# A new hand-written order of 4711 steps, and some steps on their other engine, in a one-core kernel of pooled attention and a gated dense layer

## The chip, the cores and the metric

One core of a Trainium2 chip. The time is device microseconds of one execution; "the time" of a kernel is the median of three. The engines are TensorE (PE: matrix products; PEld is its weight load), VectorE (DVE), ScalarE (ACT), GpSimd (POOL) and SyncE (SP, which only starts transfers). Each works through its own queue in order and meets the others at semaphores.

## The reference

Attention over 8 batches and 8 heads of 576 queries of 64 columns. Keys and values are averaged over 8 neighbours first, so 72 are left of each. The result, 4608 tokens by 512, goes through a dense layer of 2048 columns with a sigmoid gate and back to 512.

```python
k_p = k.reshape(B, H, Sp, pool, D).mean(axis=3)
v_p = v.reshape(B, H, Sp, pool, D).mean(axis=3)
scores = scale * np.matmul(q, k_p.transpose(0, 1, 3, 2))
attn = np.exp(scores - np.max(scores, axis=-1, keepdims=True))
attn = attn / (np.sum(attn, axis=-1, keepdims=True) + 1e-09)
x = np.matmul(attn, v_p).transpose(0, 2, 1, 3).reshape(B * S, H * D)
h = x @ w_in
g = h * (1.0 / (1.0 + np.exp(-1.702 * h)))
out = g @ w_out
```

## The kernel before

**Numbers in two halves.** PE multiplies rounded operands. To keep the precision, an operand is split into a rounded part and the rest: a copy rounds it (`x`, `ah`, `gh`), a subtraction makes the rest (`x` again, `al`, `gl`). A product is then the sum of three matmuls. So most products on PE wait for a copy (ACT or DVE) and a subtraction (DVE or POOL).

**Tiles and stages.** Batch b's first 512 tokens are chunk b of the dense layer. Chunks 0 and 1 are computed directly: `h` (lines 1675 to 1677), gate `g`, `gh`, `gl`, and `o` (1717 to 1719), each step three matmuls of 512 columns. For chunks 2 to 6 pairs of weight blocks are used with combined operands (as in Strassen's scheme): `pair` makes products `ha` and `hb` of six matmuls of 256 columns (line 1880), copies an `ha` product out of its bank into `shared` or `gall` ("keep copy", `cs`, line 1895), adds (1902), applies the gate (1919, 1927), subtracts (`gl`, 1934), and `outputs` makes `o` (2086 to 2088), in steps of three matmuls again. Chunk 7 and the 64 tokens left of every batch come last: `hidden` (`la`, `lb`, `lc`, line 2155), sums and splits of the gate's results (`ou`, line 2332; `oa`, `ob`, `oc`, `od`, lines 2323 and 2326), `outgoing` (`m1` to `m7`, line 2386), and `combined`, which adds and stores.

**Attention beside it.** The attention of batch b+1 runs between the products of chunk b, in two pieces of 256 and 320 tokens and blocks of 128 of the 512 columns. For a piece: scores (line 1126), exponent, sums, weighing `sc` (1198), copies of the weights into `main` (1241) and `tail` (1232), a transpose of each on DVE (`mt`, 1341; `tt`, 1290), splits `ah`/`al` and `at` (1348, 1353, 1311, 1314), and the product with the values `pav` (1365 to 1368) into one of two PSUM banks. From the bank DVE or ACT read: a copy `xt` (1425), the rounded `x` (1413) and the rest `x` (1416). From the `xt` of the two pieces combinations are subtracted (`less`, 1457) and split (1463), the operands `x` and `xs` of the pair products. The pooled keys of the next batch come from a reduction `red` (908), `tred` (970), masks `kbd`, `tbd` (918, 980) and a product `kps` (1004). The weights' own splits and sums are `stage` (1787, 1790).

**The order.** All 4711 steps are made first. A string `ORDER` (lines 27 to 462) then names each once; `E:name` with E one of A (ACT), V (DVE), G (POOL), P (PE), D (load, started by SP), O (output transfer). A star in front puts the step on its other engine: a copy of ACT on DVE, a subtraction of POOL on DVE. So each engine's queue is the sequence of its tokens, and nothing is reordered behind that:

```python
for token in ORDER.split():
    engine, name = token.lstrip("*").split(":")
    t = named[f"{ENGINES[engine]} {name}"]
    assert t.before <= done, t.name
    if token[0] == "*":
        t.swap()
    placed.append(t)
    done.add(t)
```

A name like `ha5_3#1` is the second `ha` step of chunk 5's pair 3; `x2_0#0` is block 0 of batch 2, first piece (`2_0`) or second (`2_1`), of the attention.

Of the kernel before, what the change touches and what calls it, by code (L numbers as in the profile page):

```python
# [18 lines left out]
P = 128  # L19
# [22 lines left out]
P:h0_0#1 P:h0_0#2 A:w#6 P:h0_0#3 D:raw#18 P:h0_0#4 A:w#3 P:h0_0#5 A:e#10 V:nm0_1#2 G:raw#8 V:sc0_1#1 V:e#10  # L42
A:qt0_1#3 A:raw#10 G:w#6 P:h0_0#6 G:w#3 P:h0_0#7 V:raw#10 V:sc0_1#2 P:sps0_1#3 A:w#8 P:h0_0#8 P:h0_0#9 A:sc0_1#0
P:h0_0#10 A:g0_0#0 D:raw#22 P:h0_0#11 V:nm0_1#3 V:sc0_1#3 D:qr1_0#7 P:h0_0#12 V:sps0_1#0 P:h0_0#13 *A:gh0_0#0
G:raw#7 G:w#8 G:raw#10 *G:gl0_0#0 D:raw#21 A:sc0_1#1 *A:w#10 P:h0_0#14 D:qr1_0#5 *A:w#5 D:kv1_0#1 G:w#10 P:h0_0#15
D:raws#2 V:sps0_1#1 P:h0_0#16 A:g0_0#1 V:sps0_1#2 V:main0_1#1 P:h0_0#17 A:gh0_0#1 G:w#5 P:h0_0#18 A:e#9 D:tl1#0
D:raws#1 A:raw#9 P:h0_0#19 V:tail0_1#0 A:w#7 P:o0_0#0 P:o0_0#1 V:main0_1#0 P:h0_0#20 V:main0_1#2 D:raw#19 P:h0_0#21
P:h0_0#22 P:tpt0_1#0 P:apt0_1#0 G:gl0_0#1 P:o0_128#0 P:o0_128#1 D:kv1_0#0 V:e#9 A:ah0_1#0 A:at0_1#1 V:raw#9
*A:at0_0#1 A:e#11 D:raw#26 P:apt0_1#1 A:ah0_1#1 G:w#7 A:raw#11 P:h0_0#23 A:g0_0#2 V:main0_1#3 P:pav0_1#0 V:e#11
# [2487 lines left out]
```

## Time and profile before

| | us |
|---|---|
| median of three runs (877.99 to 878.96) | 878.79 |
| span of the profiled execution | 876.5 |
| PE busy | 867.8 |
| DVE busy | 712.3 |
| ACT busy | 529.5 |
| POOL busy | 318.0 |

The profiled span lies 2.3 us under the median of the timed runs, which count a little time on either side of it. The granted clock of PE is 1.00 in nearly every slice of the span. A PE row's length is that of one matmul or of a run of like ones, whose ends overlap the next; so a lost fraction of a microsecond shows in the distance between starts, and only a longer one in "idle before". DVE, ACT and POOL rows give length and start of each instruction.

### The profile page before, as it was taken

How to read it: one execution, taken by the hardware profiler on the slowest of the kernel's cores; microseconds unless marked ns; L12 is line 12 of the kernel's file. 1: busy time of each engine (PE TensorE's matmuls, PEld its weight loads, DVE VectorE, ACT ScalarE, POOL GpSimd, SP SyncE). 2: the span in 40 equal slices, each digit the busy share in tenths (PEclk: the TensorE clock that was granted, in tenths of full speed). 3: DMA queues.
4: the chain of work that ended last, by engine and by line, in shares of the span. 5: the costliest groups of instructions: out<-in, count | busy, mean ns of one | idle time of the engine just before them, and what ended most of it. 6: DMA issues, size and time to landing. Idle time of an engine off the chain costs nothing.

```text
span 876.5 us, 15636 instructions
## 1 busy us (share of the span) xinstructions
PE 867.8 (99%) x5322; PEld 775.8 (89%) x5322; DVE 712.3 (81%) x1413; ACT 529.5 (60%) x1170; POOL 318.0 (36%) x325
## 2 busy tenths in 40 slices
PE   8999999999999999999999999999999999999998
PEld 7889888888898999998999999999999988889998
DVE  6999988897879896788887877788878866778887
ACT  4987855547565774767566755677476743455430
POOL 2778753554321113222522242324522123432321
PEclk9999999999999999999999999999999999999999
DMA  9966444576577666756785777667766457978003
GB/s 275 377 219 185 131 133 162 167 228 199 173 226 218 213 209 211 232 159 209 239 245 160 219 215 231 191 200 213 213 200 194 155 182 217 332 230 298 1 13 85
DMA packets 146351, 174.31 MB, mean 199 GB/s; under 512 B 85216, under 2 KB 97504, under 8 KB 146272
## 3 DMA queue, kind: packets, MB, share of 16 engines
q1 hardware_dynamic: 141808, 165.32, 61.1%
q10 hardware_dynamic: 4464, 8.00, 2.5%
q8 instruction: 42, 0.69, 0.3%
q14 instruction: 37, 0.30, 0.1%
HBM read 141.95 MB, written 31.33 MB: 198 GB/s over the span
## 4 chain that ended last, share of the span: by engine, by line
PE 92%; SPq 2%; DVE 2%; DMA 2%; ACT 1%; issue 0%; POOL 0%; POOLq 0%; DVEq 0%; ACTq 0%
PE ha L1880 13%; PE hb L1880 10%; PE m L2386 9%; PE o L2086 8%; PE o L2087 8%; PE o L2088 8%; PE la L2155 5%; PE sps L1126 4%; PE h L1677 3%; PE h L1675 3%; PE h L1676 3%; PE o L1717 3%; PE o L1718 3%; PE o L1719 3%; PE lc L2155 2%; PE lb L2155 1%
## 5 line engine op out<-in xcount | busy, mean ns | idle before, releaser
L1934 POOL TENSOR_TENSOR glall<-shared,ghall 128x256 fp32r<-128x256 f32 x78 | 61.6, 795 | 200.2 <-ACT shared L1927 137.7
L2086 PE MATMUL o<-w,ghall 128*128 128x512 f32 x320 | 127.1, 397 | 0.0
L2087 PE MATMUL o<-w,ghall 128*128 128x512 f32 x320 | 126.2, 394 | 0.0
L2088 PE MATMUL o<-w,glall 128*128 128x512 f32 x320 | 124.9, 390 | 0.0
L2088 PEld LDWEIGHTS o<-w,glall 128*128 128x128 f32 x320 | 60.1, 188 | 13.8 <-DVE glall L1934 0.2
L1880 PE MATMUL ha<-xs,ws 128*128 128x256 f32 x480 | 70.9, 283 | 0.0
L1934 POOL TENSOR_TENSOR glall<-gall,ghall 128x256 fp32r<-128x256 f32 x43 | 33.4, 782 | 102.4 <-ACT gall L1927 73.1
L1880 PEld LDWEIGHTS ha<-xs,ws 128*128 128x128 f32 x480 | 66.2, 190 | 4.4 <-ACT gall L1895 0.2
L1880 PE MATMUL hb<-x,ws 128*128 128x256 f32 x480 | 67.1, 283 | 0.0
L2086 PEld LDWEIGHTS o<-w,ghall 128*128 128x128 f32 x320 | 60.6, 189 | 6.4
L2087 PEld LDWEIGHTS o<-w,ghall 128*128 128x128 f32 x320 | 60.6, 190 | 5.8
L1880 PEld LDWEIGHTS hb<-x,ws 128*128 128x128 f32 x480 | 63.3, 190 | 2.4
L1919 ACT ACTIVATE ghall<-shared 128x256 fp32r<-128x256 f32 x108 | 43.8, 416 | 34.8 <-DVE shared L1902 15.7
L1675 PE MATMUL h<-x,w 128*128 128x512 f32 (+1 forms) x160 | 57.5, 359 | 0.0
L1705 POOL TENSOR_TENSOR gl<-g,gh 128x512 fp32r<-128x512 f32 x27 | 36.6, 1354 | 57.3 <-ACT gh L1697 49.0
L1676 PE MATMUL h<-x,w 128*128 128x512 f32 (+1 forms) x160 | 55.5, 347 | 0.0
L1677 PE MATMUL h<-x,w 128*128 128x512 f32 (+1 forms) x160 | 55.5, 347 | 0.0
L1241 ACT COPY main<-sc 32x256 f32<-32x256 f32 (+2 forms) x109 | 48.6, 446 | 4.9 <-DVE sc L1198 2.5
L1902 DVE TENSOR_TENSOR shared<-shared,hb 128x256 f32<-128x256 f32 x81 | 33.4, 413 | 22.2 <-PE hb L1880 18.5
L1895 ACT COPY shared<-ha 128x256 f32<-128x256 f32 x63 | 23.3, 369 | 42.4 <-PE ha L1880 42.1
L1126 PE MATMUL sps<-k,qt 128*128 128x144 f32 x320 | 45.9, 287 | 0.0
L1717 PE MATMUL o<-w,gh 128*128 128x512 f32 x112 | 45.4, 405 | 0.0
(270 smaller groups left out, 2430.6 us busy)
## 6 DMA issues: line engine op xcount, KB each, us to landing
ws<-wd SPq DMA_DIRECT2D x144, 512.0 KB
shared<-wd SPq DMA_DIRECT2D x48, 256.0 KB
wd<-stage SPq DMA_DIRECT2D x16, 512.0 KB
raw<-in_moe_w_in_dram SPq DMA_DIRECT2D x15, 512.0 KB
raw<-in_moe_w_out_dram SPq DMA_DIRECT2D x15, 512.0 KB
kv_False<-in_k_dram SPq DMA_DIRECT2D x28, 256.0 KB
kv_True<-in_v_dram SPq DMA_DIRECT2D x28, 256.0 KB
out_dram<-osb ACTq DMA_DIRECT2D x28, 256.0 KB
```

The costliest lines, as they stand in the source:

```text
L1126: nc.tensor.matmul(ps()[:, t * PW : (t + 1) * PW], lhsT=qt()[:, s0 : s0 + P], rhs=m.k2()[:, jj], start=True, stop=True,)
L1675: nc.tensor.matmul(o, lhsT=w[:, 0, j], rhs=xs[:, 0], start=j == 0, stop=False)
L1676: nc.tensor.matmul(o, lhsT=w[:, 1, j], rhs=xs[:, 0], start=False, stop=False)
L1677: nc.tensor.matmul(o, lhsT=w[:, 0, j], rhs=xs[:, 1], start=False, stop=j == NJ - 1)
L1717: nc.tensor.matmul(o, lhsT=gh()[:, i, tok], rhs=w[:, 0], start=f == 0, stop=False)
L1880: nc.tensor.matmul(o, lhsT=wv()[:, r, jj], rhs=xo(k, jj), start=start and n == 0, stop=n == len(terms) - 1,  skip_group_check=not start,)
L1934: engine.tensor_tensor(out=gl(), in0=part(i), in1=gh().bitcast(F32), op=ALU.subtract)
L2086: nc.tensor.matmul(o(), lhsT=gh()[:, tok], rhs=w()[:, 0], start=start, stop=False)
L2087: nc.tensor.matmul(o(), lhsT=gh()[:, tok], rhs=w()[:, 1], start=False, stop=False)
L2088: nc.tensor.matmul(o(), lhsT=gl()[:, tok], rhs=w()[:, 0], start=False, stop=stop)
L2155: nc.tensor.matmul(bank(), lhsT=wv()[:, r, jj], rhs=xs[jj]()[:, k], start=start and n == 0, stop=n == len(terms) - 1, skip_group_check=not ...
L2386: nc.tensor.matmul(banks[i]()[:, i], lhsT=av(r)[:, i * P : (i + 1) * P], rhs=tv(k), start=p == 0 and n == 0 and (i == 0 or banks[0] is not ...
```

## The change

The string `ORDER` is replaced. The first 420 tokens are the same ones; from there on nearly every queue has a new order, though few steps move far: of PE's 1205 steps 438 keep their place and the rest move by up to 13 places, on DVE by up to 29, on ACT by up to 47, on POOL by up to 4; of the 653 loads 114 keep their place, the others move by up to 31. The stars change too: steps on DVE go from 1389 to 1377, on ACT from 1110 to 1085, on POOL from 319 to 356. All code but the string is the same, and since the string is seven lines shorter, line numbers behind it are smaller by 7 in the new file. A line of the diff, from each side:

```diff
-P:qps0_0#3 P:sps0_0#2 V:e#2 D:kv0#6 D:kv0#7 D:q0_2#0 A:raw#2 A:qt0_0#3 V:sc0_0#1 V:raw#2 D:q0_1#1 P:sps0_0#3 A:e#4
+P:sps0_0#2 V:e#2 D:kv0#6 D:kv0#7 D:q0_2#0 A:raw#2 A:qt0_0#3 V:sc0_0#1 V:raw#2 D:q0_1#1 P:sps0_0#3 A:e#4 D:q0_1#0
```

Three places, as the engines' queues stand before and now.

DVE around batch 2, beginning with the copy `xt` of the second `pav` product; before:

```order
L1425 COPY xt2_0_2499<-pav2_0_1_2469 128x256
L1241 COPY main2_1_2518<-sc2_1_2292 32x3x4x2x16 x2
L908 TENSOR_REDUCE red3_k0_2537<-kv3_0_False_2109 128x128
L1416 TENSOR_TENSOR x2_2465<-pav2_0_1_2469,x2_2465 128x256
L1241 COPY main2_1_2518<-sc2_1_2292 32x4x2x16
L1353 TENSOR_TENSOR al2_0_2_2574<-mt2_0_2_2506,ah2_0_2_2566 128x256
L1416 TENSOR_TENSOR x2_2465<-pav2_0_0_2460,x2_2465 128x256
L918 TENSOR_TENSOR kbd3_2594<-red3_k0_2537,mask2i_84 128x256
L970 TENSOR_REDUCE tred3_1_2599<-tl3_1_2278 128x64
L1241 COPY main2_1_2518<-sc2_1_2292 32x4x2x16
L1290 STREAM_TRANSPOSE tt2_1_2620<-tail2_1_2516 64x320
```

and now, beginning with the same copy:

```order
L1418 COPY xt2_0_2500<-pav2_0_1_2476 128x256
L1346 TENSOR_TENSOR al2_0_2_2558<-mt2_0_2_2502,ah2_0_2_2556 128x256
L911 TENSOR_TENSOR kbd3_2566<-red3_k0_2519,mask2i_84 128x256
L963 TENSOR_REDUCE tred3_1_2568<-tl3_1_2299 128x64
L973 TENSOR_TENSOR tbd3_2373<-tred3_1_2568,mask4_86 128x256
L1406 CAST x2_2576<-pav2_0_3_2571 128x256
L1283 STREAM_TRANSPOSE tt2_1_2596<-tail2_1_2535 64x320
L1783 TENSOR_TENSOR stage_1742<-stage_1742 128x512
L1234 COPY main2_1_2523<-sc2_1_2269 32x4x2x16
L1409 TENSOR_TENSOR x2_2576<-pav2_0_3_2571,x2_2576 128x256
L1409 TENSOR_TENSOR x2_2472<-pav2_0_0_2467,x2_2472 128x256
```

The subtraction `x2<-pav2_0_0`, which reads the bank of the first `pav` product, stood right behind `al2_0_2`; it now stands eight instructions further on, behind `tt2_1`. The copy `xt2_0<-pav2_0_1`, the first row of both, has gone behind the reduction `red3`, the other subtraction `x` and four `main` copies.

PE around pair 3 of chunk 5: `ha` and `hb` products and `o` steps of three matmuls; before:

```order
L1880 MATMUL ha5_2_6541<-x5_6309,shared8_2524 128x256 x6
L2086 MATMUL o5_0_6380<-w1_4_727,ghall0_2892 128x512
L2087 MATMUL o5_0_6380<-w1_4_727,ghall0_2892 128x512
L2088 MATMUL o5_0_6380<-w1_4_727,glall0_2945 128x512
L1880 MATMUL ha5_3_6663<-x5_5750,ws5_3_0_6475 128x256 x6
L1880 MATMUL hb5_2_6565<-xs5_14_6218,ws5_2_2_6402 128x256 x6
L2086 MATMUL o5_128_6457<-w1_4_727,ghall0_2892 128x512
L2087 MATMUL o5_128_6457<-w1_4_727,ghall0_2892 128x512
L2088 MATMUL o5_128_6457<-w1_4_727,glall0_2945 128x512
L2086 MATMUL o5_384_6426<-w1_5_829,ghall1_2956 128x512
```

and now:

```order
L1873 MATMUL ha5_2_6523<-x5_6310,shared8_2443 128x256 x6
L2079 MATMUL o5_0_6369<-w1_4_727,ghall0_2877 128x512
L2080 MATMUL o5_0_6369<-w1_4_727,ghall0_2877 128x512
L2081 MATMUL o5_0_6369<-w1_4_727,glall0_2988 128x512
L1873 MATMUL ha5_3_6656<-x5_5712,ws5_3_0_6621 128x256 x6
L1873 MATMUL hb5_2_6561<-xs5_14_6238,ws5_2_2_6407 128x256 x6
L1873 MATMUL ha5_3_6656<-xs5_15_6285,ws5_3_2_6601 128x256 x6
L2079 MATMUL o5_128_6409<-w1_4_727,ghall0_2877 128x512
L2080 MATMUL o5_128_6409<-w1_4_727,ghall0_2877 128x512
L2081 MATMUL o5_128_6409<-w1_4_727,glall0_2988 128x512
L1873 MATMUL hb5_3_6723<-x5_5793,ws5_3_0_6621 128x256 x6
```

The step `o5_128` that stood behind `hb5_2` has made room for another product into an `ha` bank: two `ha5_3` products now have one `hb` product between them.

POOL at the end, before the last m6 products; before:

```order
L2332 TENSOR_TENSOR ou0_3_9884<-store3_0_8828 128x256
L2326 TENSOR_TENSOR oa0_2_1_9952<-store2_0_8667,oa0_2_0_9843 128x512
L2332 TENSOR_TENSOR ou0_2_1_9920<-store2_0_8667,ou0_2_1_9920 128x256
L2332 TENSOR_TENSOR ou0_4_0_9993<-store4_0_8869 128x256
L2326 TENSOR_TENSOR oc0_4_1_10082<-ou0_4_0_9993,oc0_4_0_10079 128x512
L2332 TENSOR_TENSOR ou0_6_1_10189<-ou0_6_0_10116,store6_0_9121 128x256
L2326 TENSOR_TENSOR oc0_6_1_10193<-ou0_6_0_10116,oc0_6_0_10155 128x512
L2326 TENSOR_TENSOR od0_7_10191<-ou0_7_10140,od0_7_10191 128x512
```

and now:

```order
L2319 TENSOR_TENSOR od0_4_10156<-ou0_4_1_10002,od0_4_10156 128x512
L2325 TENSOR_TENSOR ou0_7_10170<-store7_0_9184 128x256 x2
L2325 TENSOR_TENSOR ou0_6_1_10190<-ou0_6_0_10159,store6_0_9126 128x256
L2325 TENSOR_TENSOR ou0_6_1_10190<-store6_0_9126,ou0_6_1_10190 128x256
L2319 TENSOR_TENSOR ob0_5_10113<-store5_0_9041,ob0_5_10113 128x256
L2319 TENSOR_TENSOR od0_7_10220<-ou0_7_10170,od0_7_10220 128x512
L2319 TENSOR_TENSOR ob0_7_10225<-store7_0_9184,ob0_7_10225 128x256
L2319 TENSOR_TENSOR od0_6_10206<-ou0_6_1_10190,od0_6_10206 128x512
L2319 TENSOR_TENSOR ob0_6_10223<-store6_0_9126,ob0_6_10223 128x256
```

`od0_6` and both `ob` subtractions of the last two blocks stand on POOL; before, they were among DVE's.

## Rows read from the trace of the kernel before

**Rows 1.** The page's busy time by engine (share of the span) and count of instructions.

```profile
PE 867.8 (99%) x5322; PEld 775.8 (89%) x5322; DVE 712.3 (81%) x1413; ACT 529.5 (60%) x1170; POOL 318.0 (36%) x325
```

**Rows 2.** Windows: stretch, its length, busy us by engine (instructions), granted clock, DMA share, GB/s.

```profile
200.00:240.00 40.00, 39.32 (x192) 33.02 (x191) 31.79 (x57) 27.67 (x59) 14.97 (x12) 1.00 0.54 179
240.00:590.00 350.00, 349.94 (x2248) 317.89 (x2247) 279.91 (x581) 227.53 (x550) 94.75 (x109) 1.00 0.70 211
...
620.00:830.00 210.00, 210.00 (x1257) 187.52 (x1256) 161.74 (x342) 114.36 (x254) 61.90 (x71) 1.00 0.63 204
```

**Rows 3.** List of PE's waits: line, releaser; us in total, times, longest.

```profile
PE pav L1365 <- DVE xt L1425: 0.7, 1, 0.7
```

**Rows 4.** Timeline of PE: start, length, engine, line, operation [idle before, releaser].

```profile
227.09 0.39 PE L1719 MATMUL o<-w,gl 128*128 128x512 f32 x1
228.15 0.41 PE L1365 MATMUL pav<-ah,vh 128*128 128x320 f32 x1 [0.68 <-DVE xt L1425]
...
600.67 0.88 PE L1880 MATMUL ha<-x,shared 128*128 128x256 f32 x6
601.38 0.88 PE L1880 MATMUL hb<-xs,ws 128*128 128x256 f32 x6
602.34 0.97 PE L1880 MATMUL ha<-x,ws 128*128 128x256 f32 x6
```

**Rows 5.** Timeline of DVE in batch 2's second piece.

```profile
208.58 2.36 DVE L1198 TENSOR_TENSOR sc<-sc,sm 128x1728 f32<-128x1728 f32 x1
...
212.31 1.10 DVE L1241 COPY main<-sc 32x384 f32<-32x384 f32 x2
213.42 2.02 DVE L908 TENSOR_REDUCE red_k<-kv_False 128x128 f32<-128x1024 f32 x1
...
215.80 0.98 DVE L1241 COPY main<-sc 32x128 f32<-32x128 f32 x1
...
217.45 0.42 DVE L1416 TENSOR_TENSOR x<-pav,x 128x256 fp32r<-128x256 f32 x1
...
218.24 1.08 DVE L970 TENSOR_REDUCE tred<-tl 128x64 f32<-128x512 f32 x1
219.35 0.22 DVE L1241 COPY main<-sc 32x128 f32<-32x128 f32 x1
220.49 0.50 DVE L1290 STREAM_TRANSPOSE tt<-tail 64x320 f32<-64x320 f32 x1 [0.92 <-ACT tail L1232]
...
225.10 0.49 DVE L1353 TENSOR_TENSOR al<-mt,ah 128x320 fp32r<-128x320 f32 x1
...
227.08 0.68 DVE L1790 TENSOR_TENSOR stage<-stage 128x512 fp32r<-128x512 f32 x1
```

**Rows 6.** Timeline of PE there: the first matmuls of two pav products.

```profile
217.47 0.28 PE L1365 MATMUL pav<-ah,vh 128*128 128x256 f32 x1
...
220.69 0.28 PE L1365 MATMUL pav<-ah,vh 128*128 128x256 f32 x1
```

**Rows 7.** Timeline of ACT there.

```profile
209.89 0.63 ACT L1787 CAST stage<-stage 128x512 fp32r<-128x512 f32 x1
...
212.00 0.30 ACT L1241 COPY main<-sc 32x128 f32<-32x128 f32 x1 [0.70 <-DVE mt L1341]
...
220.19 0.27 ACT L1232 COPY tail<-sc 32x96 f32<-32x96 f32 x1
```

**Rows 8.** Instructions of lines 1457 and 2326: ns min/median/max, first and last start.

```profile
L1457 DVE TENSOR_TENSOR xt<-xt,xt x6: 685/691/1775, 236.7 to 616.7; 128x512 f32<-128x512 f32 x6
...
L2326 POOL TENSOR_TENSOR ob<-store,ob x3: 742/857/921, 763.3 to 832.7; 128x256 fp32r<-128x256 f32 x3
...
L2326 POOL TENSOR_TENSOR od<-ou,od x2: 1469/1631/1793, 830.9 to 862.8; 128x512 fp32r<-128x512 f32 x2
```

**Rows 9.** Timelines of POOL and of DVE near the end.

```profile
861.53 1.29 POOL L2326 TENSOR_TENSOR oc<-ou,oc 128x512 fp32r<-128x512 f32 x1
...
861.60 1.50 DVE L2332 TENSOR_TENSOR ou<-store,ou 128x256 f32<-128x256 f32 x1 [0.63 <-POOL ou L2332]
```

More of the change, by code (lines that the diff above doesn't have):

```diff
@@ new lines @@
+*G:stage0_2#0 V:x1_0#1 D:wd1_0#0 P:h0_0#63 G:stage0_0#0 G:stage#1 D:tl2_1#0 A:g0_0#10 A:gh0_0#10 V:at1_1#1 V:qt2_0#1
+V:at1_1#0 P:pav1_1#0 A:x1_1#0 A:left1_1#0 P:apt1_1#1 A:ah1_1#1 *G:gl0_0#10 P:warm0_0#6 *G:stage0_3#0 D:kv2_0#2
+G:stage#7 G:stage#8 P:o0_0#13 P:o0_0#14 V:kbd2#1 D:wd6_3#0 V:x1_1#0 D:qr2_0#14 A:g0_0#11 A:gh0_0#11 V:al1_1#1
+P:pav1_1#1 A:left1_1#1 D:tl2_1#3 V:tred2_1#0 P:apt1_1#2 A:ah1_1#2 *G:stage#6 V:tbd2_1#0 G:stage#9 *A:stage#2
+*G:stage#2 P:o0_256#14 P:o0_128#14 D:wd7_0#0 P:h1_0#4 D:wd5_0#0 D:qr2_0#10 D:wd4_3#0 A:x1_1#1 V:x1_1#1 P:h1_0#0
@@ new lines @@
+D:wd5_3#0 P:h1_0#36 P:o1_384#7 P:h1_0#37 P:o1_128#7 P:h1_0#38 P:h1_0#39 D:qr3_0#2 A:gh1_0#8 D:ws2_0#2 D:wd0_3#0
+D:qr3_0#3 V:nm2_1#2 V:nm2_1#3 V:sc2_1#2 G:stage#37 *G:stage#30 V:sc2_1#3 G:stage#38 *G:stage#39 V:tbd3_0#0 D:kv3_0#1
+D:qr3_0#0 V:qt3_0#0 V:al2_0#1 V:mt2_0#0 G:gl1_0#8 P:o1_384#8 P:o1_0#8 G:stage#33 A:stage#10 P:h1_0#40 P:h1_0#41
+A:g1_0#9 A:gh1_0#9 P:h1_0#44 P:h1_0#42 P:h1_0#45 P:o1_256#8 D:wd6_0#0 D:tl3_1#3 P:o1_128#8 D:qr3_0#6 D:tl3_1#0
+D:qr3_0#4 D:wd2_0#0 D:qr3_0#7 D:1_1#0 D:qr3_0#5 G:stage#36 A:stage#12 G:stage#40 D:wd6_1#0 D:tl3_1#1 P:h1_0#43
@@ new lines @@
+*A:main3_0#4 V:mt3_0#0 *A:tail3_0#7 *A:ah3_0#0 V:vbd3#1 A:vh3#0 G:stage#42 D:qr3_1#14 *A:stage#14 *G:stage#46
+A:gh2_2#2 A:cs2_2#6 G:gl2_2#0 *G:gl2_2#2 V:al3_0#0 P:o2_0#4 P:ha2_3#1 V:cs2_3#0 *A:cs2_3#1 V:vt3#0 *G:gl2_2#1
+A:gh2_2#3 A:cs2_2#7 P:o2_128#4 P:ha2_3#2 A:cs2_3#3 D:ws2_4#3 P:sps3_1#0 *A:tail3_0#0 D:tl4_0#0 *G:vl3#0 A:tail3_0#6
+V:tt3_0#0 A:at3_0#0 A:at3_0#1 D:ws2_5#0 D:ws2_4#2 D:ws2_5#1 V:qt3_1#3 V:qt3_1#2 V:nm3_1#1 P:o2_384#4 P:o2_0#5
+P:o2_256#4 G:gl2_2#3 P:o2_256#5 P:ha2_3#3 A:cs2_3#4 A:gh2_3#0 D:2_1#0 A:cs2_3#2 V:nm3_1#0 V:cs2_3#1 A:gh2_3#2
@@ new lines @@
+A:cs2_3#6 G:gl2_3#2 V:red4_0#0 P:o2_384#5 *A:stage#15 V:sc3_1#0 P:ha2_4#0 *A:cs2_4#0 V:sc3_1#1 V:at3_0#1 P:o2_128#5
+P:hb2_3#2 P:sps3_1#1 A:gh2_3#1 *G:gl2_3#0 V:at3_0#0 V:cs2_3#2 V:mt3_0#1 A:ah3_0#1 A:cs2_3#5 P:ha2_4#1 G:gl2_3#1
+D:ws2_5#2 P:o2_256#6 P:hb2_4#0 D:qr4_0#3 V:al3_0#1 V:kbd4#0 G:stage#47 A:gh2_3#3 A:cs2_3#7 V:nm3_1#2 V:sc3_1#2
+D:qr4_0#6 D:qr4_0#5 V:mt3_0#2 V:nm3_1#3 P:o2_384#6 P:pav3_0#0 V:sc3_1#3 *A:ah3_0#2 A:cs2_4#1 P:ha2_4#2 A:cs2_4#3
+P:hb2_4#1 V:cs2_4#1 D:ws2_6#0 P:ha2_4#3 P:o2_128#6 G:gl2_3#3 P:o2_0#6 A:sc3_1#0 V:al3_0#2 P:pav3_0#2 P:o2_128#7
@@ new lines @@
+A:main6_0#14 D:qr6_1#15 A:cs5_2#7 A:tail6_0#7 A:main6_0#15 D:ws5_4#2 D:ws5_4#1 A:main6_0#13 P:ha5_3#1 A:cs5_3#1
+P:o5_128#4 *A:tail6_0#2 A:main6_0#4 *A:main6_0#7 V:mt6_0#0 *A:tail6_0#4 A:ah6_0#0 D:ws5_4#3 A:tail6_0#6 V:al6_0#0
+*A:tail6_0#5 V:tt6_0#0 A:at6_0#0 D:ws5_4#0 P:hb5_3#0 P:hb5_3#1 V:cs5_3#0 G:gl5_2#1 P:o5_0#5 P:ha5_3#2 *A:cs5_3#3
+P:sps6_1#0 A:gh5_3#0 A:cs5_3#2 *G:gl5_3#0 V:at6_0#0 V:nm6_1#0 P:o5_384#4 V:cs5_3#1 V:nm6_1#1 V:qt6_1#3 V:sc6_1#0
+V:sc6_1#1 P:o5_256#4 G:gl5_2#3 P:o5_384#5 P:o5_256#5 P:o5_128#5 P:ha5_3#3 D:qr6_1#10 P:hb5_3#2 V:qt6_1#2 D:qr7_0#6
```

818 lines of the change are left out of this document (393 added, 425 removed).

## The prediction

> **What bounds the kernel now.** I read the busy shares first, then TensorE's (PE's) idle time by stretch, then the places where PE starts late. PE is busy for 867.8 of 876.5 us and the next engine, VectorE (DVE), for 712.3 [rows 1]. Behind the common first steps, which end at about 73 us, hardly anything is left: PE shows 39.32 busy of 40 us between 200 and 240, 349.94 of 350 between 240 and 590, and 210.00 of 210 between 620 and 830 [rows 2]. The one wait that the list of PE's waits shows there is `pav` for a copy `xt` on DVE, 0.7 us [rows 3]. A second, shorter one shows only in start times: the products of six matmuls that begin at 600.67 and 601.38 stand 0.71 apart, but the one after them begins 0.96 after the second, so 0.25 were lost [rows 4]. And the `pav` at 228.15 starts 1.06 after the 512-column matmul in front of it, where such matmuls stand 0.23 apart (0.68 for three, below): 0.83 lost [rows 4]. What the order can still give behind the first steps is therefore about 0.83 + 0.25 + 0.06 = 1.1 us (0.06 is the idle time between 240 and 590). Between the last product and the end of the span come the last additions and the output transfers, whose order and engines stay as they are.
>
> **The change, part by part.** It edits nothing but the string that fixes the order. PE gets the same products in another order, so its own work stays as it is: 0. The time can only move by waits that PE gains or loses, and by 1.1 us at most downwards. "Within 0.2%" means within 1.76 us here, about what a measurement of this kernel can tell from no change.
>
> *Batch 2, second piece (205 to 240 us).* Here the code lets one queue decide. The `pav` products of one piece use two banks in turn, so the third product must wait until DVE or ScalarE (ACT) has read the first's bank: by the copy `xt`, the rounded `x` and the subtraction `x` minus rounded `x`. Before, DVE makes this subtraction for block 0 at 217.45 [rows 5], and the product that needs it starts at 220.69 [rows 6]: 2.82 us of slack. After, eight DVE instructions stand between it and its old neighbour, among them the transpose `tt`, and `tt` waits for the last of ACT's eight tail copies. I add this up from the rows of before.
>
> DVE first. The weighing `sc` ends at 208.58 + 2.36 = 210.94, and four short operations follow until 212.31, the copy `xt` the last of them [rows 5]. The first three stay, until about 211.9. Then, in the new order: `red3` 2.02, a 128x256 subtraction 0.42, two `main` copies 1.10, a third `main` copy (0.98 in before, a like one further on takes 0.22; I count 0.3 to 0.98), a fourth 0.55, and only now the copy `xt`, 0.4 [rows 5]. That ends at 216.6 to 217.3. The fourth `pav` (the first one of this stretch), which waits for that copy, now stands one step of three matmuls earlier: between 217.47 and 220.69 lie four steps and a `pav`, so 0.68 a step, and it is due at 216.79 [rows 6]. Its wait is 0 to 0.5. Behind the copy come `al` and `kbd` (each like the 0.42 of a 128x256 operation), `tred` 1.08, `tbd` and a rounding (0.4 each): 219.3 to 220.0. Then `tt`.
>
> ACT: before, the last tail ends at 220.46, and `tt` starts right behind it, after 0.92 of idle time on DVE for that very reason; ACT had begun the run of copies, gelu steps and one rounding that ends there at 212.00 [rows 5, 7], so it took 8.46. In the new queue one tail (0.27) and the rounding of a weight tile (0.63, made earlier before) stand in this run as well, one `main` copy (0.53, like the 0.55 above) no longer: 8.83, from the same start: 220.8. So `tt` starts at about 220.85, no matter how soon DVE comes to it. Behind it DVE has `tt` 0.50, a subtraction of weights `stage` 0.68, a `main` copy 0.22, and two subtractions of 0.42 [rows 5], 2.24 less some overlap: 223.0. The third `pav`, now a step later, is due at 220.69 + 0.68 = 221.37 [rows 6]. **PE waits 1.6 us** in all. The next `pav` waited 0.83 before. Its inputs end with the subtraction `al`, in before at 225.59, 5.10 after `tt` began [rows 5]; now `stage`, one subtraction and one copy more lie between: 220.85 + 5.10 + 0.68 + 0.42 + 0.4 = 227.45. PE, which stood ready at 228.15 - 0.83 = 227.32, has two steps (1.36) less ahead of it and 1.6 of waiting more: 227.56. So that wait is gone, by a narrow margin. Behind that, the pooled-key product of batch 3 wants three DVE subtractions that now stand behind a reduction of 2.0 us: 0.05 to 0.45 more, I take 0.2. Net: 1.6 + 0.2 - 0.83 = **+1.0**. From below: if the tails end that much sooner than I sum, nothing is lost and 0.83 gained (-0.8). From above: one DVE operation slowed as far as rows 8 show (1.08 more) gives +2.1.
>
> *Short distances between the keep copy and the product that reuses its bank (240 to 720 us).* An `ha` product is copied out of its bank, and the next product into this bank can't start before. The old order leaves only one other product or one o step between (0.65 to 0.72 us of PE work) at 13 such places, the new one at 28, in a row of three around `ha5_3`. Of the 13 one lost 0.25 (the place of rows 4), one 0.05, the others nothing that start times show. Fifteen more places at this mean of 0.02 are **+0.3**; the ends are 0, and 15 x 0.25 = 3.7, which would need the copying engine to be taken at every one of them. I take the mean, since 11 of 13 cost nothing.
>
> *Batch 6 (594 to 616 us).* The combinations `xs` and `x` of the last pair chunk share POOL and DVE, and several of them have changed places. By the rows' medians POOL's are there just about when PE wants them: 0 to 0.5; one slowed subtraction on DVE (1.775 instead of 0.691, [rows 8]) gives 1.1. I take **+0.2**.
>
> *The end (848 to 868 us).* The last subtractions `ob` and `od` move from DVE to POOL. The chain from one m4 product to an m6 product is: copy 0.41 to 0.6, `ob` 0.74 to 0.92, `od` 1.47 to 1.79 [rows 8], 2.6 to 3.3 us; between the two on PE lie four products of 0.71 to 0.72 [rows 4], 2.88. Wait 0 to 0.5; I take **+0.1**.
>
> *Elsewhere.* Subtractions go both ways between POOL and DVE (37 more on POOL in the end), copies between ACT and DVE, and loads at other places of SyncE's queue. Cover: behind 73 us no PE wait for a load stands in the list, and DVE is busy 280 of 350 us between 240 and 590 [rows 2], so a queue that slips recovers within a few steps. The 0.25 at 602 may go: **-0.2**. Without cover each place costs what it slips, some tenths.
>
> Sum: 1.0 + 0.3 + 0.2 + 0.1 - 0.2 = +1.4. On the profiled execution's own span, 876.5, that is 877.9. The median of before, 878.79, stands 2.3 above that span, time outside it that no order changes. Forecast **880.2 us**.
>
> **A row that speaks against the change.** DVE subtractions of 128x512 take 0.691 us in the median but 1.775 at most [rows 8]. One of 128x256, 0.42 as a rule [rows 5], took 1.50 where a POOL subtraction had begun 0.07 ahead of it [rows 9]. Both are 1.08 longer. The new order has 356 steps on POOL where the old has 319, so there is more to collide with. *The Trainium skill, "SBUF — State Buffer", section "Who interferes with whom", says that a DVE instruction with two SBUF inputs and a GpSimd instruction that reads SBUF exclude one another, and the later one stands still until the first is done. The pair in rows 9 agrees with that: the excess of 1.08 fits into POOL's 1.29.* By the medians alone the sum stays at 880.2; with such collisions at two places that PE is due for it is rival (b)'s 882.7.
>
> **Rivals.**
> (a) *The waits only change places.* ACT has its tails out sooner than my sum (its copies overlap by a few hundredths each) and the batch-2 wait comes to what the old one was: +0.2 with the rest, 879.0. For it: 11 of 13 short places cost nothing, and PE showed 210.00 of 210 in a stretch as crowded as the new ones. Against it: `tt` waits for a tail in the old order too, with 0.92 us idle on DVE [rows 5], and the new order puts the bank's reader behind it.
> (b) *Slower: POOL holds DVE.* Each of the two stretches in which DVE feeds PE directly (batch 2 and batch 6) has one DVE operation held for 1.08 us, and two of the new short places lose 0.25 each: 1.4 - 0.2 (batch 6, priced anew) + 2 x 1.08 + 0.5 = +3.9, 882.7. It decides as soon as POOL starts within 0.4 us ahead of a DVE subtraction that PE is due for. For it: rows 8 and 9. Against it: the slowed operations of before cost PE nothing that its waits show [rows 3].
> (c) *Faster:* all 1.1 us of waits go and no new one shows: 877.7. For it: the `pav` wait of 228 does go in my sum. Against it: the new order's own queue at `tt`.
>
> **How the numbers follow.** Forecast 0.45 (880.2; its terms spread by about 1 us to either side, so some three eighths of it lie beyond +1.76), (a) 0.18, (b) 0.26, (c) 0.11. Faster by over 0.2% would take 1.76 us where 1.1 are to be had, so only part of (c), with gains that no row shows: 0.05. Slower: all of (b) and 0.17 of the forecast: 0.43. Within: 0.28 + 0.18 + 0.06 = 0.52. The range 878.0 to 883.5 leaves out most of (c) and the worst of (b).
>
> **What would show it.** In the new profile: a PE wait of 1 to 2 us near 221, for a DVE operation that stands behind `tt`; no wait, or a short one, at the next `pav` near 228; PE's busy time in 240 to 590 and 620 to 830 lower by a few tenths, in pieces of 0.05 to 0.25 in front of `ha` products; at most 0.5 lost in front of an m6 product near 867. The forecast is wrong if the batch-2 stretch has PE at 39.5 or more of 40 (then (a) or (c)), or if single DVE subtractions of over 1 us stand just in front of PE waits (then (b)), or if PE's own start-to-start times differ, which I hold for excluded.

## The result, and the profile after

The new kernel takes 891.53 us (median of four runs, 891.09 to 891.71); the kernel before, run beside it, took 878.47. The ratio is 1.0146, 95% interval 1.0133 to 1.0159: 13 us slower, where the forecast was 880.2 and its range ended at 883.5.

The busy times of the page, as in [rows 1], and the windows of [rows 2] (stretch, its length, busy us by engine, granted clock):

```profile
PE 874.8 (98%) x5322; PEld 774.4 (87%) x5322; DVE 724.3 (81%) x1401; ACT 524.4 (59%) x1145; POOL 359.3 (40%) x362
```

```profile
200.00:240.00 40.00, 37.88 (x179) 31.35 (x178) 32.02 (x54) 26.65 (x56) 16.23 (x13) 1.00 0.49 155
240.00:590.00 350.00, 347.33 (x2207) 311.28 (x2206) 278.52 (x589) 221.86 (x522) 88.55 (x101) 1.00 0.68 207
620.00:830.00 210.00, 208.13 (x1202) 182.49 (x1201) 163.45 (x318) 112.01 (x251) 91.44 (x96) 1.00 0.67 216
```

PE runs the same 5322 matmuls at the same clock. Between 240 and 590 it is idle 2.67 us instead of 0.06, between 620 and 830 1.87 instead of 0. The list of PE's waits from 74 to 712 us, which held one row in before [rows 3] (line, releaser; us in total, times, longest), now reads:

```profile
PE ha L1873 <- ACT shared L1888: 1.4, 3, 0.7
PE pav L1358 <- DVE x L1409: 1.4, 1, 1.4
PE h L1668 <- ACT gh L1690: 1.2, 2, 0.8
PE o L2081 <- POOL glall L1927: 1.0, 4, 0.4
PE pav L1358 <- ACT ghall L1912: 0.6, 1, 0.6
PE ha L1873 <- ACT gall L1888: 0.4, 1, 0.4
PE ha L1873 <- DVE shared L1888: 0.3, 1, 0.3
PE pav L1358 <- DVE sc L1150: 0.2, 1, 0.2
PE ha L1873 <- DVE gall L1888: 0.2, 1, 0.2
PE sps L1119 <- DVE qt L1103: 0.2, 1, 0.2
```

These rows add up to 6.9 us, about half of the loss. A wait costs more than its idle time, as one place shows (PE: start, length, line, idle before and releaser):

```profile
408.97 0.39 PE L2081 MATMUL o<-w,glall 128*128 128x512 f32 x1
410.07 0.98 PE L1873 MATMUL ha<-xs,ws 128*128 128x256 f32 x6 [0.71 <-ACT shared L1888]
410.88 0.40 PE L2079 MATMUL o<-w,ghall 128*128 128x512 f32 x1
```

The idle time is 0.71, but the starts stand 1.10 apart where 0.23 is the rule: 0.87 lost, since the matmul in front counts as busy while it drains. The six matmuls behind the wait then take 0.81 to the next start instead of 0.72: 0.09 more, a restart. So I counted by starts, against the median distance of the same pair of lines. Behind 74 us PE loses 20.1 us in the new kernel and 6.8 in before; the difference, 13.3, is the whole difference of the spans (889.8 and 876.5). Of it 10.1 lies between 245 and 712 us and 3.1 between 160 and 245. PE's own work is unchanged.

Of the 20.1 us, 26 waits of 0.13 to 1.52 us make 11.5, where before has four that make 1.4; the rest are restarts of about 0.1 and a floor of hundredths that before has too. By what PE waits for: 14 are `ha` and `hb` products that wait for a keep copy or an addition (4.9 us in all, between 279 and 710), four are `o` steps that wait for POOL's `gl` (1.6), four belong to batch 2's second piece and the last direct steps ahead of it (`h1_0#20` .63, `h1_0#52` .92, `pav2_0#2` 1.52, `kps3_0#0` .16), and four are attention steps elsewhere (1.8). Behind 710 us there is none.

**Batch 2.** PE, DVE, ACT and POOL there (start, length, line, idle before):

```profile
167.97 0.50 PE L1668 MATMUL h<-x,w 128*128 128x512 f32 x1 [0.47 <-ACT gh L1690]
...
217.96 0.50 PE L1668 MATMUL h<-x,w 128*128 128x512 f32 x1 [0.76 <-ACT gh L1690]
...
224.89 0.35 PE L1358 MATMUL pav<-ah,vh 128*128 128x256 f32 x1 [1.36 <-DVE x L1409]
```

```profile
209.79 1.92 DVE L1191 TENSOR_TENSOR sc<-sc,sm 128x1728 f32<-128x1728 f32 x1
211.63 1.51 DVE L1346 TENSOR_TENSOR al<-mt,ah 128x256 fp32r<-128x256 f32 x1
...
213.40 0.43 DVE L1334 STREAM_TRANSPOSE mt<-main 128x256 f32<-128x256 f32 x1
...
222.67 0.50 DVE L1283 STREAM_TRANSPOSE tt<-tail 64x320 f32<-64x320 f32 x1 [0.82 <-ACT tail L1225]
```

```profile
209.94 2.92 POOL L1698 TENSOR_TENSOR gl<-g,gh 128x512 fp32r<-128x512 f32 x1 [1.74 <-ACT gh L1690]
```

```profile
165.53 1.28 ACT L1685 ACT_TABLE_LOAD   x1 [2.04 <-PE h L1670]
...
213.91 0.53 ACT L1234 COPY main<-sc 32x384 f32<-32x384 f32 x1 [2.98 <-DVE mt L1334]
...
217.31 0.60 ACT L1690 ACTIVATE gh<-h 128x512 fp32r<-128x512 f32 x1
```

The wait at 224.89 is the one foretold: `x` of block 0 behind `tt`, and `tt` for a tail copy. Ahead of it `al` took 1.51 us instead of 0.42 [rows 5] beside POOL's `gl`; it ended 0.28 behind POOL's end. *The Trainium skill, "SBUF — State Buffer", section "Who interferes with whom", lets a DVE instruction with two SBUF inputs stand still until a GpSimd instruction that reads SBUF is through; this row agrees.* That `gl` had itself begun 0.15 behind DVE's `sc` and took 2.92 us, where the median of its like is 1.30. Behind `al` the transpose `mt` came some 1.1 us late. For it ACT stood idle 2.98 us at a `main` copy, and from 213.91 on it worked without a gap through the `gh` of 217.31 to the last tail copy before `tt`. The two `h` waits were not foretold. Both are for ACT's gelu copies: the first pays a table load of 1.28 us that ACT begins only after 2.04 us of idle time; the second waits for the `gh` of 217.31. So the held `al` stands behind the 0.92 and behind a part of the 1.52. With ACT's run 1.1 us earlier the `h` product would not wait and the `pav` would wait about 1.3, which puts the hold at some 1.1 us of PE's time. This is an estimate from these rows; no run took the hold away.

### The profile page after: what moved, and what is told of

Its sections match the earlier page's. It is cut to its first block, busy times and chain, and to the rows that moved or that the text cites. A ratio compares the mean times of both kernels' runs of the same rounds, so it can differ in the third digit from the quotient of the medians.

```text
span 889.8 us, 15557 instructions
## 1 busy us (share of the span) xinstructions
PE 874.8 (98%) x5322; PEld 774.4 (87%) x5322; DVE 724.3 (81%) x1401; ACT 524.4 (59%) x1145; POOL 359.3 (40%) x362
## 5 line engine op out<-in xcount | busy, mean ns | idle before, releaser
L1927 POOL TENSOR_TENSOR glall<-shared,ghall 128x256 fp32r<-128x256 f32 x71 | 56.2, 797 | 181.3 <-ACT shared L1920 123.7
L1927 POOL TENSOR_TENSOR glall<-gall,ghall 128x256 fp32r<-128x256 f32 x41 | 31.6, 776 | 136.6 <-ACT gall L1920 112.8
L1698 POOL TENSOR_TENSOR gl<-g,gh 128x512 fp32r<-128x512 f32 x27 | 39.1, 1448 | 61.1 <-ACT gh L1690 33.5
L1920 ACT ACTIVATE shared<-shared 128x256 f32<-128x256 f32 x108 | 44.5, 417 | 5.2 <-DMA ws<-wd 1.4
```

The costliest lines, as they stand in the source:

```text
L1927: engine.tensor_tensor(out=gl(), in0=part(i), in1=gh().bitcast(F32), op=ALU.subtract)
```

## How a helper comes late: one place

The 0.87 us at 410 show what happens along the whole stretch. ACT and DVE of the new kernel there:

```profile
407.06 0.42 ACT L1912 ACTIVATE ghall<-shared 128x256 fp32r<-128x256 f32 x1 [0.86 <-DVE shared L1888]
407.50 1.08 ACT L1234 COPY main<-sc 32x384 f32<-32x384 f32 x2
408.60 0.42 ACT L1912 ACTIVATE ghall<-shared 128x256 fp32r<-128x256 f32 x1
409.04 0.27 ACT L1225 COPY tail<-sc 32x96 f32<-32x96 f32 x1
409.34 0.42 ACT L1920 ACTIVATE shared<-shared 128x256 f32<-128x256 f32 x1
409.66 0.35 ACT L1888 COPY shared<-ha 128x256 f32<-128x256 f32 x1
```

```profile
407.00 0.67 DVE L1225 COPY tail<-sc 32x96 f32<-32x96 f32 x3
409.35 0.50 DVE L1283 STREAM_TRANSPOSE tt<-tail 64x320 f32<-64x320 f32 x1 [1.68 <-ACT tail L1225]
409.88 1.11 DVE L1234 COPY main<-sc 32x384 f32<-32x384 f32 x2
411.02 0.42 DVE L1895 TENSOR_TENSOR gall<-gall,hb 128x256 f32<-128x256 f32 x1
```

ACT stands 0.86 us at a gelu copy whose input DVE hasn't made, while the tail copy four places behind it has had its input since 402.1. DVE then stands 1.68 us at `tt` for that tail copy, while the addition `cs3_5#2` of the last row, whose product ended at 406.56, waits three instructions behind. And on ACT the keep copy of the last row, whose product ended at 408.67, queues behind all this until 409.66; PE waits for it. No engine is short of time: in these three microseconds each stands idle for the other. In before, ACT began five tails of the same piece one after the other from 398.8 to 399.9, and `tt` began at 407.00 without a wait.

Over 74 to 712 us the waits of the helpers changed in kind. First before, then the new kernel:

```profile
DVE shared L1902 <- PE hb L1880: 18.5, 22, 2.6
DVE shared L1895 <- PE ha L1880: 15.5, 23, 1.4
...
DVE at L1314 <- ACT at L1311: 1.7, 4, 0.5
...
DVE tt L1290 <- ACT tail L1232: 1.5, 2, 0.9
```

```profile
...
DVE shared L1888 <- PE ha L1873: 9.1, 11, 1.8
...
DVE at L1307 <- ACT at L1304: 4.8, 7, 1.3
DVE shared L1895 <- PE hb L1873: 4.3, 8, 1.5
DVE tt L1283 <- ACT tail L1225: 3.8, 5, 1.7
```

A helper that waits for PE is early: this is slack. A helper that waits for another helper blocks all that stands behind it in its queue. Summed over gaps above 0.1 us by releaser, DVE's idle time for PE falls from 67.4 to 47.4 us and ACT's from 144.2 to 114.1, while ACT's idle time for DVE rises from 58.9 to 93.7 and DVE's for ACT from 35.3 to 53.6.

## The experiments

The edits are to the order string; the diffs show the tokens of one queue. Ratios are to the kernel before, run beside them.

**Which part of the change.** First the engines alone and the order alone: 274 steps change engine in all.

```diff
 old_order_new_engines: the old sequence, the new stars
- A:cs2_3#0 ... *G:gl2_2#0 ...
+ *A:cs2_3#0 ... G:gl2_2#0 ...
 new_order_old_engines: the new sequence, the old stars
```

> The old order of all 4711 steps, but every step on the engine that the new string gives it (37 more subtractions on POOL, the stars of the new string). Theory E (engines): DVE is held by POOL more often (slowed DVE operations sum to 62 us instead of 45 in the two traces) and the 13 us come from that: this kernel is 5 to 13 us slower than the old one. Theory Q (queues): the 13 us are steps that stand behind others in their queue when PE comes to them; with the old order only single places suffer, 0 to 4 us slower.

> The new order, but every step on the engine that the old string gives it. Theory E: most of the 13 us go, 879 to 884. Theory Q: the queues stay as crowded in front of the same products, 888 to 895.

Measured: 894.86, ratio 1.0192 (1.0177 to 1.0207), and 908.44, ratio 1.0350 (1.0334 to 1.0365). All four expectations were missed. Neither part is the culprit: each alone is worse than both together. With the engines alone, two waits behind 712 us make 6.5 of the loss, and both are gone in the new kernel:

```profile
PE la L2149 <- ACT store L2161: 3.3, 1, 3.3
PE m3b L2380 <- DVE store L2421: 3.2, 1, 3.2
```

Next, PE's queue alone in the new order from `ha2_1#0` to `o6_128#11`, all others old.

```diff
 old_with_new_pe_order: PE's queue, chunks 2 to 6 (251 of 1205 steps moved)
- old sequence
+ new sequence
```

> The old order on ACT, DVE, POOL and the transfer queues throughout; only PE's queue is in the new order, and only from the first product ha2_1#0 (250 us) to o6_128#11 (some 690 us). If PE's own order (28 instead of 13 short distances to a bank in use) makes the waits of this stretch, 8 to 10 of the 13 us lie there and this kernel is 5 to 10 us slower than the old one. If the order on ACT and DVE makes them, it is within 2 us of the old one.

Measured: 901.88, ratio 1.0275 (1.0260 to 1.0290), with waits up to 2.56 us by starts; both expectations were missed. PE's new order with the helpers' old one is far worse than either whole order, so PE's order can't be judged by its own queue. The other way round, PE's old order with the helpers' new one, was not run.

**Which stretch.** The new kernel with a stretch of the old order and its engines put back, and the old with the new end:

```diff
 new_with_old_batch2: 488 steps, 160 to 245 us
 new_with_old_middle: 2643 steps, 245 to 712 us
 old_with_new_end: the last 679 steps, from la7_0#0 on (POOL 99 steps there instead of 55)
- new (or old) sequence of the stretch
+ old (or new) sequence of the stretch
```

> The new kernel, but the 488 steps of one stretch (about 160 to 245 us, from h1_0#13 to the second score product of batch 3) stand in the old order on their old engines. In the new trace this stretch loses 0.63 (h1_0#20), 0.92 (h1_0#52), 1.52 (pav2_0#2) and some tenths behind them, in the old one 0.83 at a pav. If each place's loss stands alone, 2.5 to 3.5 us come back: 888 to 889. If the time is given back later (PE comes sooner to the next late copy), less than 1 us comes back.

> The new kernel with the 2643 steps from the score products of batch 3 (about 245 us) to just before la7_0#0 (about 712 us) in the old order on their old engines. In the new trace 20 of the 24 waits behind the first steps lie in this stretch. If they all come from the order in it, only the losses of batch 2 are left: 880 to 882. If something from outside the stretch (loads, the extra POOL steps at the end) takes part, it stays above 884.

> The old kernel with the last 679 steps, from la7_0#0 on (about 711 us to the end), in the new order and on the new engines: 99 steps on POOL there instead of 55. The new trace shows no wait of PE behind 710 us. Theory E (POOL work costs time) expects 2 us or more on top of the old time; theory Q expects the old time, within 0.5 us.

Measured: 889.25, 1.0129 (1.0112 to 1.0146); 881.04, 1.0039 (1.0024 to 1.0054); 879.12, 1.0017 (1.0008 to 1.0026). So the middle holds some 10 us of the 13, as expected, and batch 2 some 2, between its two expectations. The new end costs 1.5 with the old order ahead of it, which neither theory has. In the first of these the other waits came back at the same places and nearly all within 0.05 us: the loss isn't chance, it is written in the queues. The end has all of POOL's additional steps (44 more there, 4 fewer in the middle), so POOL's load isn't what the middle suffers from.

**Single steps.** Three edits take the late steps one by one: 14 keep copies and additions moved ahead of one to four small copies, ten PE steps exchanged with their neighbours so that the copy has more time, and `x2_0#0` moved ahead in front of the `pav` of 224.89.

```diff
 new_keep_earlier, ACT:  tail4_1#1 gh3_5#1 main4_1#2 main4_1#8
+  cs3_6#0
   gh3_5#2 tail4_1#3 cs3_5#5
-  cs3_6#0
 new_far, PE:  ha3_6#0 o3_384#9
-  ha3_6#1 o3_128#10
+  o3_128#10 ha3_6#1
 new_x2_ahead, DVE:  al2_0#2
+  x2_0#0
   kbd3#0 tred3_1#0 tbd3_1#0 x2_0#3 tt2_1#0 stage#35 main2_1#14 x2_0#3
-  x2_0#0
```

> The new kernel with 14 copies or additions out of a product's bank moved ahead of one to four small copies in their own queue on ACT or DVE; PE's order and all engines as in the new kernel. In the new trace PE waits for just these 14, for 4.8 us plus about 0.1 us at each place behind it. Theory Q (they stand too far back in their queue): 4 to 6 us come back, 885.5 to 887.5. Theory D (the distance on PE is too short as such): the copies can't come soon enough, less than 1.5 us comes back. If the small copies that now run later are waited for in their turn, it is in between, with new waits in front of pav and sps.

> The new kernel with PE's queue changed at 10 of these places only: the product that waits for its bank changes places with the step behind it, so that the copy has 0.5 to 0.7 us more. They lose 3.5 us and some tenths behind each in the new trace. Theory D or Q alike: 3 to 4.5 us come back if what moves ahead is ready itself, 887 to 888.5. If PE only meets the next late input, less than 1.5 us.

> The new kernel with one step moved: the DVE subtraction x2_0#0 goes ahead of kbd3, eight places forward, so that it no longer stands behind the transpose tt. The wait of 1.52 us in front of pav2_0#2 must go. Theory L (each place's loss stands alone): 1.3 to 1.7 us come back, 890. Theory G (given back): the chain over tt stays as it is, PE comes to the next pav (pav2_1#1) 1.5 us sooner and waits there for it, 0 to 0.5 us come back, 891 to 891.5.

Measured: 890.20, 1.0141 (1.0127 to 1.0155); 893.21, 1.0172 (1.0158 to 1.0185); 891.19, 1.0150 (1.0136 to 1.0163). Each edit removes nearly all of the waits that it aims at, and others come close by; new_far, where 3 to 4.5 us or a little were expected back, loses about 2 more. In new_keep_earlier the 0.87 at `ha3_6#1` is gone, and the next product loses 1.35:

```profile
410.78 1.70 PE L1873 MATMUL hb<-x,ws 128*128 128x256 f32 x12 [1.19 <-DVE gall L1895]
```

```profile
408.63 0.50 DVE L1283 STREAM_TRANSPOSE tt<-tail 64x320 f32<-64x320 f32 x1 [2.20 <-ACT tail L1225]
```

It waits for the addition that stands behind the blocked `tt`; with PE earlier, `tt` blocks for 2.20 instead of 1.68. In new_x2_ahead the 1.52 goes and 0.85 comes at the next `o` step, for POOL's `gl1_0#12`; the time is theory G's, the place is not the `pav` that it names.

**Load.** If DVE were simply too full, less work on it would mend the waits. 24 of its reductions read two of eight neighbours.

```diff
- out=red(), in_=raw().rearrange("p i (w d) -> p i d w", w=POOL), ...
+ out=red(), in_=raw()[:, :, 0 : 2 * D].rearrange("p i (w d) -> p i d w", w=2), ...
```

> The new kernel, but the 24 DVE reductions that pool the keys and values of batches 2 to 7 read two of eight neighbours only (0.55 us instead of 2.0), so that DVE has some 35 us less to do between 115 and 650 us; nothing else is changed. Theory L (DVE's queue as a whole runs late in these stretches, whichever step stands first): 4 to 8 of the 13 us come back. Theory P (each wait comes from the few steps just ahead of the late one in its own queue): less than 2 us.

> The old kernel with the same 24 reductions over two of eight neighbours. Its waits behind the first steps come to 1.3 us in all: at most that comes back, 876.5 to 878.

Measured: 891.09, 1.0151 (1.0136 to 1.0166), and 877.29, 0.9996 (0.9987 to 1.0006). The new kernel's page with the lighter sums:

```profile
PE 875.0 (98%) x5322; PEld 776.0 (87%) x5322; DVE 688.2 (77%) x1401; ACT 524.3 (59%) x1145; POOL 358.6 (40%) x362
```

DVE has 36 us less to do, and the time is the same. Of 24 waits of at least 0.15 us, 21 come back within 0.05. The theory of load falls. *The Trainium skill, "Perfetto Trace Analysis", section "Optimization Strategies", advises to optimize the engines that hold up the matmul engine; here 36 us less work on one of them brought nothing.* What its order brought is told next.

**Blocked heads.** Two theories were left: (1) the head of a helper's queue waits for the other helper while ready work for PE stands behind it, or (2) PE's new order is itself too close to its helpers. To tell them apart I let the measured durations run through the queues (each step starts when its engine is free and its inputs are there) and moved steps of ACT and DVE alone.

```diff
 new_tail_one, ACT:  main4_1#5 x4_0#3 tail4_1#1 gh3_5#1
+  tail4_1#3
   main4_1#2 main4_1#8
+  cs3_6#0
   gh3_5#2
-  tail4_1#3
   cs3_5#5
-  cs3_6#0
```

> The new kernel with two copies moved ahead on ACT and nothing else: tail4_1#3 (0.27 us, its input ready since 402.1 us) two places ahead, in front of main4_1#2, and keep copy cs3_6#0 in front of gh3_5#2. Theory (a blocked head): DVE's 1.68 us of idle time in front of tt4_1#0 goes, so the additions behind it run in time: the wait of .87 us at ha3_6#1 goes, and no wait comes at hb3_6#0, where moving cs3_6#0 alone had left 1.35 us. All other waits stay as they are to some hundredths. Time 0.8 to 1.0 us under the new kernel's, 890.6. Rival (each wait that is mended comes back a few steps later, because the helpers are late as a whole): a wait of .5 us or more at hb3_6#0, o3_128#10 or the pav products behind it, time within 0.3 us of 891.5.

At the place, the blocked head is shown: PE and DVE there now read

```profile
412.31 0.93 PE L1873 MATMUL ha<-xs,ws 128*128 128x256 f32 x6
...
413.77 1.59 PE L1873 MATMUL hb<-x,ws 128*128 128x256 f32 x12
```

```profile
410.89 0.50 DVE L1283 STREAM_TRANSPOSE tt<-tail 64x320 f32<-64x320 f32 x1
```

The idle time in front of `tt` is gone, `ha` and the `hb` behind it start without a wait, and the other waits of the middle return at their places. The time doesn't settle it: 890.74, ratio 1.0159 (1.0143 to 1.0175), where 0.1% was at stake. Its profiled execution lost 1.43 us at `ha2_2#0` besides, where ACT stood over 2 us at the start of an output transfer; the same happened in the profiled execution of the next run, whose span is 883.7 while the other three have 881.0 to 881.4.

```diff
 new_helpers_freed: 13 of 1085 ACT steps and 24 of 1377 DVE steps moved by one to four places, PE and POOL as in new; for instance
 ACT:  main7_0#13
-  gh6_2#0
   tail7_0#3 cs6_2#3
+  gh6_2#0
 DVE:  mt3_0#1
-  al3_0#1
   kbd4#0 nm3_1#2 sc3_1#2
+  al3_0#1
 new_all_freed: 30 steps of ACT and DVE, and 16 of PE
 old_freed: the same done to before: 13 steps of ACT and DVE, and 6 of PE
```

> The new kernel with TensorE's and GpSimd's queues untouched, and 37 of the 2462 steps in ACT's and DVE's queues moved by one to four places: steps that stood at the head waiting for another engine, while a copy or addition that TensorE needed next stood ready behind them, change places with it. Worked out by letting the durations of the new kernel's trace run through the queues (each step starts when its engine is free and its inputs are there), the waits of TensorE behind 74 us fall from 13.5 to 2.9 us, at pav2_0#2 1.0, ha4_6#0 .31, ha5_3#2 .28. Theory (blocked heads in the helpers' queues, not TensorE's order and not load): 881 us, range 879.5 to 883.5, with 2 to 4 real waits over .25 us left. Rival (TensorE's new order is itself too close to its helpers): most waits move elsewhere, as they did when 14 copies were moved ahead, 888 to 891.

> As new_helpers_freed, and TensorE's queue may change too: 30 steps of ACT and DVE and 16 of TensorE's 1205 moved by one to four places. The durations of the new kernel's trace, run through these queues, leave 1.3 us of waits. Theory: 879.5 us, range 878 to 882, so 1.5 us less than new_helpers_freed. Rival: 887 to 891.

> The kernel before, mended in the same way: 13 steps of ACT and DVE and 6 of TensorE moved by one to five places. The durations of its trace leave 0.1 of 0.8 us of waits (this working doesn't see the .84 us at pav2_1#1). Theory: 0.7 to 1.6 us under the kernel before, so 876.2 to 877.1, and 2 to 4 us under the best of the new order. Rival (the old order has nothing to mend, new waits come for those that go): within 0.3 us of the kernel before.

Measured: new_helpers_freed 883.07, 1.0064 (1.0048 to 1.0079); new_all_freed 882.71, 1.0063 (1.0049 to 1.0077); old_freed 875.85, 0.9981 (0.9972 to 0.9989). With PE's queue untouched, 37 moved steps take the loss against before from 1.46% to 0.64%: 7 of 13 us, within the range expected. So the order of ACT's and DVE's queues carries the larger part, and PE's new order as such at most the rest. That the blocking heads wait for the other helper is shown at single places, as at 410 us; the sums don't show it. ACT's idle time for DVE only falls from 93.7 to 86.5 and DVE's for ACT from 53.6 to 46.9, and old_with_new_pe_order, 24 us slower than before, has 74.3 and 46.0. What counts is which step stands behind the wait. PE's waits of the second profile, from 74 to 712 us:

```profile
PE ha L1873 <- DVE shared L1888: 1.3, 1, 1.3
PE h L1668 <- ACT gh L1690: 1.3, 2, 0.8
PE pav L1358 <- ACT at L1304: 0.8, 1, 0.8
PE apt L1263 <- DVE x L1409: 0.6, 1, 0.6
PE o L2081 <- POOL glall L1927: 0.5, 1, 0.5
```

The first row is the transfer told of above. Between 265 and 712 us four waits of 0.13 us or more are left, 1.1 us by starts, where the new kernel has 21 that make 8.0; `ha` and `hb` products lose 0.5 of the 1.1. With the transfer's 1.43 left out, the loss over before between 245 and 712 us falls from 10.1 to 2.2. What remains lies mostly ahead of 265: besides the transfer's there are seven waits that make 3.9 us, some of them new, and `al` is held for 1.51 us there as in the new kernel. Over the whole execution at least five waits above 0.25 us are left besides the transfer's, where 2 to 4 were expected. Freeing PE's order as well (16 steps) brought nothing more that the intervals can tell: both expectations for it, 878 to 882 and 887 to 891, were missed, the first by 0.7. The rest of the difference to before, some 5 us, is in these waits and in short restarts.

**The old order** was not without slack to give either. An earlier try mended its three longest waits by hand:

```diff
 old_mended, DVE:
+  xt2_0#3
   mt2_1#1 ...
-  xt2_0#3
 and cs2_2#3, cs2_2#1 ahead of tail3_0#7; on PE ha5_7#0 one step later
```

> The old kernel with its three waits behind the first steps mended: the copy xt2_0#3 on DVE ahead of mt2_1#1 (a 0.54 us gap of DVE), a keep copy and the addition behind it ahead of two small copies, and ha5_7#0 exchanged with the o step behind it. They lose 0.84 + 0.22 + 0.24 us and some 0.1 behind each in the old trace. Theory L: 1.0 to 1.5 us come back, a ratio of 0.9985. Theory G: less than 0.4 us, the same as before.

Measured: 877.22, 0.9990 (0.9981 to 0.9999), with a new wait of 0.38 at `ha2_3#0`. old_freed, 19 steps moved, has none: PE is busy for 171.00 of 171 us and 467.00 of 467 in the windows 74 to 245 and 245 to 712. At 875.85 it beats before by 1.65 us and the new kernel by about 1.6%; that is a little more than expected against before, and 6.9 us under the best of the new order where 2 to 4 were expected.

## Why the prediction was wrong, point by point

- **What bounds the kernel**: right. PE's work didn't change, and all 13.3 us are waits and restarts of PE. But 1.1 us was too little for what the order could still give at most: old_freed gives 1.65. Of the `hb` wait at 267.72, 0.22 by starts, only the 0.06 of idle time was counted.
- **Batch 2, +1.0**: the right place and mechanism, sized too small. The wait for `x` behind `tt` was 1.52 for 1.6 foretold, the `pav` wait of [rows 3] is gone, and the pooled-key product lost 0.16 for 0.2. That 1.52 comes so near 1.6 is in part luck, since both sides came later than summed: `tt` began at 222.67 instead of 220.85 (ACT's run was some 8.7 long for 8.83, but began at 213.91 instead of 212.00, behind the held `al`), and PE was due at 223.37 instead of 221.37. Missing were the two `h` waits, .63 and .92. The working began at 205 us and asked only who feeds `pav`; the copies of ACT that it put behind a weight tile's rounding (0.63) are the gelu copies that PE needs as well. With them the stretch is 0.63 + 0.92 + 1.52 + 0.16 - 0.84 = 2.4. new_with_old_batch2 gave back 2.
- **Short bank distances, +0.3 with an upper end of 3.7**: this term was mis-sized most. `ha` and `hb` products lose 4.9 us and a restart of about 0.1 for each of 14 waits. The price of 0.02 a place was the old queues' price: in the old order the copying engine came to its keep copies in time. How far the next product stands was the wrong question, as new_far shows, where more distance brought waits at the next steps, and new_helpers_freed, where the same distances cost 0.5 between 265 and 712 us.
- **Batch 6, +0.2**: 0.13 and 0.13 at two `ha5_6` products: right.
- **The end, +0.1**: no wait: right. With the old order ahead of it the same end costs 1.5 (old_with_new_end).
- **Elsewhere, -0.2**: the step that failed. It said that behind 73 us "a queue that slips recovers within a few steps", since DVE is busy 280 of 350 us. Busy share is no measure of that. DVE is as busy in the new middle (278.52 of 350), and new_light_sums took 36 us off it for nothing. The idle fifth isn't a reserve where it is spent in waiting for the other helper. The `gl`, attention and scores waits, 3.4 us, belong here, and so does the cause of the 4.9 above.
- **Rival (b), POOL holds DVE, 882.7**: it happened in batch 2 (`al`, 1.51) and cost PE some 1.1 us by the estimate above, so the mechanism was right for that stretch. It isn't the cause in the middle. DVE operations more than 0.05 us above the median of their kind rose from 86 to about 120, but the rise lies behind 712 us (15 to 65), where PE has no wait; between 245 and 712 they fell from 50 to 31. An edit that takes away the holds alone wasn't run.
- **Rivals (a) and (c)** fell with the sum. No rival had blocked heads along the whole stretch; the transpose `tt` waiting for a tail, which the prediction worked out for batch 2, was that mechanism, and it recurs in the pieces after it.

Could it have been foreseen? I let the durations of *before* run through both kernels' queues, after the fact. By this estimate, which no run shows, 0.8 us of waits are left in the old order and 28 in the new, at 42 places; 21 of the 26 real waits are among these, so half of the places are false and the sum is twice too large. If the estimate holds, the sign was in the rows and the size was not. Four places priced by hand were no sample of 4711 steps.

## What to carry to other kernels

When an order is rewritten by hand, follow every engine's queue through with the measured durations before pricing any place: busy shares and bank distances don't show what waits behind a blocked head. In a helper's idle time, read who ends it: a wait for the bound engine is slack; at a wait for another helper, read on to what stands behind it, for the sum of such waits doesn't measure the loss. Here late steps were mended by exchanging them with the head that blocked their queue; moving them ahead of copies that were ready (new_keep_earlier) brought about 1 us.

## What the runs showed that I had not expected

- In these traces a wait of PE costs its idle time in the list plus about 0.16 us in front and 0.1 behind: 0.71 listed, 0.96 lost.
- Waits recur at the same places within about 0.03 to 0.05 us from kernel to kernel as long as the queues there are the same, though the rest of the order differs.
- A table load of ACT (1.28 us) can stand on either side of a wait. In the new trace the gate's load stood behind idle time at five places (0.40 to 2.04 us), and at the longest PE lost 0.63, less than the load took; the exponent's load stood ahead of it at five places behind 74 us (0.37 to 1.44).
- An output transfer that ACT issues can hold its queue for over 2 us in some executions (2.39 in one), and what stood behind it then cost PE 1.43.
